# A Fourier-mixing and ELU kernel: batches 2 to 7 transformed from rows sorted by s mod 8, with the sums on VectorE

## The chip, the cores and the metric

One core of one Trainium2 chip. The metric is the device time of one execution in microseconds, lower is better. The engines are named as in the profile: PE is TensorE (matmul) and PEld its weight loads, DVE is VectorE, ACT is ScalarE, POOL is GpSimd, SP is SyncE, which here issues DMAs.

## What is computed

```python
batch, seq, dim = (8, 3008, 256)          # x, float32
X = np.fft.fft(np.fft.fft(x, axis=1), axis=2).real
h = X.reshape(8 * 3008, 256) @ w_in        # w_in  256 x 2048
g = np.where(h > 0, h, np.exp(np.minimum(h, 0)) - 1)
out = g @ w_out                            # w_out 2048 x 256
```

## The kernel before, in words

All products are float32, and each is two passes on PE. The transform over the 256 channels is multiplied into `w_in` once, which gives `Wc` (cosine part) and `Ws` (sine part). What is left of the first stage is the transform over the sequence, real and imaginary, of the channel-folded rows. Its results are written column by column (a column is one wave number) into rings `Rr` and `Ir` in SBUF, with `Rb` for one odd channel out. Wave numbers k and 3008 - k share their products: one gives the sum, the other the difference.

**The main loop.** The 8 x 1504 columns come in 47 tiles of `TW` = 256, and each tile in 8 slots, each of 256 of the 2048 hidden features: 376 slots. A slot is a fixed schedule: every piece of work is put in a list with a time in units of `T` = `PERIOD`, and the list, sorted by time, gives the order of instructions on every engine (`pin` keeps it). Slot s has, by offset from s T:

- 0: `mm_P`, two products of `Rr` into a PSUM bank H (PE).
- 0.87: `mm_X1` of slot s - 2, three products of the output matmul (PE). 0.9: `even_part`, which makes E from H, `Rb` and `wex` (DVE, line 1130).
- 2.17: `mm_Q`, two products of `Ir` added into H (PE). They add to what `even_part` reads, so they wait for E.
- 2.2 and 2.9: `g_plus`, `g_minus` of slot s - 1 (DVE, line 1160). From then on `sum_1`, `sum_3`, `sum_2`, `sum_4` of that slot run on POOL (line 576, out<-in G<-G): they are the sums of a Winograd form of the output matmul, which needs 7 products in place of 8.
- 3.04: `mm_X2`, `mm_X3` (PE). 3.55: `h_minus` (DVE, line 1144). 4.2 and 4.8: `below_plus`, `below_minus`, and in the next slot the two exponentials (ACT).
- Once in 8 slots: `comb_1` and `comb_2` at 4.2 (s mod 8 = 1), `comb_22` and `comb_3` at 1.0 and 2.5 (s mod 8 = 2), `turn_u` and `turn_v` at 4.2 (3 and 4), all on DVE, and the stores on SP's queue.

**The transforms.** Batch b covers 47 slots (`steps_b`), and while batch b - 1 goes through the main loop, batch b is loaded, folded and transformed; s0 = 47 (b - 1). Four tiles `xl0` to `xl3` take the rows s, 3008 - s, 1504 - s and 1504 + s, 6 rows to a partition. The folds (`fold_x`, line 664, on POOL in two halves each) first fold the channels, c with 256 - c (`e0` to `e3` the sums, `o0` to `o3` the differences), and then the four tiles with each other (`E0`, `E2`, `EO0`, `EO1`, `O0`, `O2`, `EO2`, `EO3`). In batches 2 to 7, `Mirror` uses rows paired by the mirror symmetry of 752: S and D, two more sums and differences on POOL, serve the odd rows of the even wave numbers. A transform has an even and an odd part, each a DFT of its own of 3 products into one bank H, put in at offset 4.75 of a slot, that is, between the slots on PE. In the next slot ACT copies a piece of it (`copy`), and DVE unfolds it (`unfold`) or joins even and odd into the ring (`plus`, `minus`), at offset 1.0, which is between E and g. There are 8 such parts a batch (real or imaginary, even or odd wave numbers, even or odd part), at s0 + 28, 30, 34, 36, 38, 40, 42 and 44. Matrices `MM` replace the earlier `MC` in the same tiles.

The helpers `mm` (line 567), `vtt` (573, DVE), `gtt` (576, POOL) and `act` (579) issue most instructions, so these lines stand for many places, and the names of the tiles tell them apart.

Of the kernel before, what the change touches and what calls it, by code (L numbers as in the profile page):

```python
# [17 lines left out]
SEQ = 3008  # L18
# [13 lines left out]
NC = (189, 188)  # L32
MW = (1417, 1786)
MOFF = (0, 1417, 3203, 4620)
# [42 lines left out]
def _row_pairs():  # L77
    p = np.arange(128)
    first = np.where(p < 96, 8 * p, 500 + 8 * (p - 96))
    second = np.where(p < 96, 750 - 8 * p, 250 - 8 * (p - 96))  # L80
    third = np.where(p < 64, 4 + 8 * p, 258 + 8 * (p - 64))
    return first, np.maximum(second, 0), third


def _used():
    p = np.arange(128)
    used = np.ones((128, 6), bool)
    used[94, 1:4] = False
    used[95, 0:4] = False
    used[:, 4] = used[:, 5] = p % 64 < 62  # L90
    return used


def _mirror_consts():

    rows = np.stack([r + o for r in _row_pairs() for o in range(2)], axis=1)
    used = _used()
    out = []
    for ri in range(2):
        fn = np.cos if ri == 0 else np.sin  # L100
        for kodd in range(2):

            def block(m, k, keep=None):
                s = rows[:, m : m + 1]
                w = np.where(s == 0, 0.5, 1.0) * used[:, m : m + 1]
                w = np.where(s == RUN, 0.5 if ri == kodd else 0.0, w)
                if keep is not None:
                    w = w * keep(s)
                return w * fn(2.0 * np.pi * ((s * k[None, :]) % SEQ) / SEQ)

            ka = 2 * np.arange(NA[kodd]) + kodd
            kc = 2 * np.arange(NC[kodd]) + kodd
            a = lambda m: block(m, ka, lambda s: s % 8 == 0)
            b = lambda m: block(m, ka, lambda s: s % 8 == 4)
            c = lambda m: block(m, kc, lambda s: s % 4 == 2)
            parts = [a(0), b(0), c(2), b(4), c(4)]
            if kodd:
                k = 2 * np.arange(NO) + 1
                parts += [block(m, k) for m in (1, 3, 5)]
            else:  # L120
                ev, od = 4 * np.arange(189), 4 * np.arange(188) + 2
                parts += [block(1, od if ri else ev), block(1, ev if ri else od)]
                parts += [block(5, ev), block(5, od)]
            out += parts
    return np.concatenate(out, axis=1).astype(np.float32)

# [35 lines left out]
def kernel(  # L162
# [14 lines left out]
    MM_dr = nc.inline_tensor(_mirror_consts(), name="mirror_mats")  # L177
# [27 lines left out]
    ix = cpool.tile([128, 7], I32, tag="ix")  # L205
# [51 lines left out]
    def mirror_table(c):  # L257

        for first, n, base in (
            ((0, 128, HALF - 1), (96, 32, HALF - 501)),  # L260
            ((0, 128, 750), (96, 32, 250)),
            ((0, 128, HALF - 5), (64, 64, HALF - 259)),
            ((0, 128, HALF - 1), (96, 32, HALF - 501), (0, 1, HALF - 2)),
        )[c]:
            pin(
                nc.gpsimd.iota(
                    ix[first : first + n, c + 3 : c + 4],
                    pattern=[[0, 1]],
                    base=base,
                    channel_multiplier=-8,  # L270
                )
            )
        if c == 1:
            pin(
                nc.vector.tensor_scalar(
                    out=ix[:, 4:5], in0=ix[:, 4:5], scalar1=0x3FF, scalar2=None,
                    op0=ALU.bitwise_and,
                )
            )

    def load_mirror(b):

        L = [
            spool.tile([128, 6 * ND], FP, tag=f"xl{j}", bufs=1, name=f"xl{j}")
            for j in range(4)
        ]

        def gather(j, pair):
            back = j in (1, 2)
            c = 3 if b == NB - 1 and j == 1 and pair == 0 else pair  # L290
            block = 2 - pair if back else pair
            pin(
                nc.gpsimd.indirect_dma_start(
                    out=L[j][:, 2 * block * ND : (2 * block + 2) * ND],
# [3 lines left out]
                        ap=ix[:, c + 3 : c + 4].bitcast(U32), axis=0  # L298
# [4 lines left out]

        def ahead(j):
            pairs = L[j].rearrange("p (m c) -> p m c", c=2 * ND)[:, 0::2]
            for p, q, row, gap in ((0, 64, 0, 4), (64, 96, 512, -254), (96, 128, 500, 14)):
                nc.sync.dma_start(
                    out=pairs[p:q],
                    in_=bass.AP(
                        tensor=xt,  # L310
                        offset=x.offset + (b * SEQ + (HALF if j else 0) + row) * ND,
                        ap=[[8 * ND, q - p], [gap * ND, 2], [1, 2 * ND]],
                    ),
                )

        def back(j):
            last = (SEQ if j == 1 else HALF) - 1
            cuts = (0, 80, 94, 128) if j == 1 else (0, 96, 128)
            for p, q in zip(cuts, cuts[1:]):
                s = 750 - 8 * p if p < 94 else 1018 - 8 * p  # L320
                nc.sync.dma_start(
                    out=L[j][p:q, 2 * ND : 4 * ND], in_=xrows(b, last - s, 8, q - p, 2)
                )

        loads = [
            lambda j=j, pair=pair: gather(j, pair)
            for j, pair in ((3, 1), (2, 0), (2, 2), (0, 1), (1, 0), (1, 2))
        ]
        loads += [
            lambda: ahead(3), lambda: back(2), lambda: ahead(0), lambda: back(1)  # L330
        ]
        return L, loads

# [201 lines left out]
    MM = {}  # L535

    def load_mirror_mats(ri, kodd):
        t = cpool.tile([128, BW], FP, tag=f"MC{ri}{kodd}", name=f"MM{ri}{kodd}")
        MM[ri, kodd] = t
        n = MOFF[2 * ri + kodd]  # L540
        nc.sync.dma_start(out=t[:, 0 : MW[kodd]], in_=MM_dr.ap()[:, n : n + MW[kodd]])

# [115 lines left out]
    def fold_x(L, engine_of, cuts_of, mirror=False, last=False):  # L658
# [36 lines left out]

        def first_row():

            if last:
                act(L[1][0:1, 4 * ND : 5 * ND], L[1][0:1, 5 * ND :])
            act(L[1][0:1, 5 * ND :], L[0][0:1, 0:ND])  # L700

        ops["x1", 0] = first_row
# [8 lines left out]
        if not mirror:  # L711
            return [E[1], E[3], O[1], O[3]], ops

        sd = []
        for n, t in ((0, E[1]), (2, O[1])):
            d = spool.tile([128, 380], FP, tag="side", bufs=2, name=f"sd{n}")
            sd.append(d)
            for m, f in ((0, ALU.add), (1, ALU.subtract)):
                op(
                    f"{'SD'[m]}{n}",  # L720
                    d[:, 128 * m : 128 * m + 128],
                    t[:, 128:256],
                    t[:, 384:512],
                    f,
                )
        return [(E[1], sd[0]), (E[3],), (O[1], sd[1]), (O[3],)], ops
# [5 lines left out]
    MIRROR_FOLDS = (  # L732
        "e0 c0 e3 c3 e2 c2 x1 e1 c1 E0 E2 EO0 S0 D0 o0 o3 o2 o1 O0 O2 EO2 S2 D2 EO1 EO3".split()
    )
# [59 lines left out]
    class Dft:  # L794
# [23 lines left out]

        def plus(self):
# [24 lines left out]
    def mirror_parts(ri, kodd, par):  # L844


        na, nc_ = NA[kodd], NC[kodd]
        if not par:
            return [
                (0, 0, 2 * na, 0),  # L850
                (2, 2 * na, nc_, 2 * na),
                (4, 2 * na + nc_, na + nc_, na),
            ]
        z = 3 * na + 2 * nc_
        if kodd:
            return [(2 * t + 1, z + t * NO, NO, 0) for t in range(3)]
        n = (188, 189) if ri else (189, 188)
        return [
            (6, z, n[0], 189 if ri else 0),
            (7, z + n[0], n[1], 0 if ri else 189),  # L860
            (5, z + NE, NE, 0),
        ]

    def of_tiles(tiles_):

        def stat(m):
            t, c = (tiles_[1], m - 6) if m > 5 else (tiles_[0], m)
            return t[:, 128 * c : 128 * c + 128]

        return stat  # L870

# [13 lines left out]
    def unfold_near(even, near, ab, ri, kodd, M, tt):  # L885


        na, nc_ = NA[kodd], NC[kodd]
        a, b, ab = even[0:M, 0:na], near[0:M, 0:na], ab[0:M]
        tt(ab[:, 0:na], a, b, ALU.add)  # L890
        p, q = (b, a) if ri else (a, b)
        tt(ab[:, steps_of(nc_ - 1, 94, -1)], p[:, 0:94], q[:, 0:94], ALU.subtract)

    def unfold_far(es, even, ab, ri, kodd, M, tt):
        na, nc_ = NA[kodd], NC[kodd]
# [6 lines left out]
    def join(es, odd, kodd, to, tt, ri=0, part=None):  # L902
# [7 lines left out]
        def run(t, start, step):  # L910
            return lambda i, z: t[:, steps_of(start + i * step, z - i, step)]
# [920 lines left out]
```

## Time and profile before

| | |
|---|---|
| median of 3 runs | 1935.96 us (1935.94 to 1936.14) |
| profiled execution, its own time | 1937.37 us |
| span from first to last instruction | 1934.6 us |
| granted TensorE clock | 1.000 |
| busy PE / PEld / DVE / ACT / POOL | 1923.9 / 1651.4 / 1305.2 / 864.3 / 1398.6 us |
| chain that ended last | PE 94%, DVE 3%, POOL 2%, ACT 1% |
| HBM read and written | 46.94 and 24.80 MB |

The busy time of an engine is the union of its instructions' times. PE's products overlap, so the time that one takes from the stream is read from start to start and not from its duration. A line of the timeline has start, duration, engine, line, operation, out<-in, shapes and count; several instructions in a row can be merged into one. In brackets stands the idle time before it and what ended it. A line of the groups has, after the shapes and the count, the busy time in us, the mean of one in ns, and the idle time before them with what ended it.

### The profile page before, as it was taken

The page shows a single profiled execution, that of the slowest core. Times are in us where ns is not written, and L with a number is a line of the kernel's source. Part 1 is how long each engine was busy: PE and PEld are TensorE (multiplying, and loading weights), DVE is VectorE, ACT ScalarE, POOL GpSimd, SP SyncE. Part 2 cuts the span into 40 slices and gives each one's busy share as a digit, 9 for nine tenths or more (in the row PEclk, how much of TensorE's full clock was granted, in tenths as well). Part 3 has the DMA queues.
Part 4 walks back from the last instruction along what each step waited for, and adds up shares of the span by engine and source line. Part 5 has one row for each costly group of instructions (what it writes and reads, how often), then busy time and mean ns, then how long its engine had stood idle before and what let it go on. Part 6 is the DMA issues. An engine that isn't in the chain of part 4 may idle for free.

```text
span 1934.6 us, 27221 instructions
## 1 busy us (share of the span) xinstructions
PE 1923.9 (99%) x8912; PEld 1651.4 (85%) x8912; DVE 1305.2 (67%) x2475; ACT 864.3 (45%) x1672; POOL 1398.6 (72%) x1860
## 2 busy tenths in 40 slices
PE   9999999999999999999999999999999999999999
PEld 6788788888888888888888888888888888888887
DVE  8876666766666666666666666676666666667666
ACT  5644444444444444444444444444444444444443
POOL 4888767876778777787677876778767876556555
PEclk9999999999999999999999999999999999999999
DMA  8146221111111111010110202012020110100101
GB/s 335 44 34 47 55 81 35 37 26 30 38 20 34 27 38 34 19 43 17 43 35 13 46 15 54 17 20 59 7 53 12 20 23 15 17 12 13 22 11 24
DMA packets 266141, 73.55 MB, mean 38 GB/s; under 512 B 249406, under 2 KB 250322, under 8 KB 266000
## 3 DMA queue, kind: packets, MB, share of 16 engines
q1 hardware_dynamic: 260048, 58.97, 15.6%
q0 software_dynamic: 3776, 12.59, 2.0%
q8 instruction: 70, 1.15, 0.2%
q14 instruction: 71, 0.58, 0.1%
q10 hardware_dynamic: 2176, 0.26, 0.1%
HBM read 46.94 MB, written 24.80 MB: 37 GB/s over the span
## 4 chain that ended last, share of the span: by engine, by line
PE 94%; DVE 3%; POOL 2%; ACT 1%; issue 1%; DMA 0%; DVEq 0%; POOLq 0%
PE H L567 37%; PE pB L567 16%; PE pC L567 16%; PE pD L567 16%; PE pA L567 8%; POOL WT L576 1%; POOL G L576 1%; DVE G L1160 0%; DVE E L1130 0%; DMA xl<-in_x_dram,ix 0%; DVE v L573 0%; DVE u L573 0%; DVE e L664 0%; POOL w L576 0%; DVE G L1144 0%
## 5 line engine op out<-in xcount | busy, mean ns | idle before, releaser
L576 POOL TENSOR_TENSOR G<-G 128x256 f32<-128x256 f32 x1440 | 1036.5, 730 | 479.9 <-DVE G L1160 364.1
L1130 DVE SCALAR_TENSOR_TENSOR E<-Rb,wex,H 128x256 f32<-128x256 f32 x752 | 327.9, 477 | 524.0 <-PE H L567 521.0
L579 ACT ACTIVATE G<-H 128x512 f32<-128x512 f32 x376 | 224.7, 598 | 958.1 <-DVE G L1144 953.5
L567 PE MATMUL H<-Ir,Ws 128*128 128x256 f32 x1504 | 387.4, 380 | 2.0 <-DVE E L1130 1.9
L567 PE MATMUL H<-Rr,Wc 128*128 128x256 f32 x1504 | 387.0, 380 | 0.8 <-DVE Ir L573 0.8
L567 PE MATMUL pC<-G,WT 128*128 128x256 f32 x1440 | 369.5, 379 | 0.0
L567 PEld LDWEIGHTS H<-Rr,Wc 128*128 128x128 f32 x1504 | 284.7, 190 | 52.2 <-issue 2.2
L567 PEld LDWEIGHTS H<-Ir,Ws 128*128 128x128 f32 x1504 | 278.5, 189 | 50.8 <-DVE E L1130 5.8
L567 PEld LDWEIGHTS pC<-G,WT 128*128 128x128 f32 x1440 | 273.6, 190 | 37.2
L1144 DVE SCALAR_TENSOR_TENSOR G<-E,H 128x512 f32<-128x512 f32 x376 | 257.1, 684 | 42.8 <-POOL G L576 4.0
L1160 DVE SCALAR_TENSOR_TENSOR G<-G,H 128x512 f32<-128x512 f32 x376 | 256.3, 682 | 43.1 <-ACT G L579 43.1
L1160 DVE SCALAR_TENSOR_TENSOR G<-M,G 128x512 f32<-128x512 f32 x376 | 257.3, 684 | 0.4 <-ACT M L579 0.4
L579 ACT ACTIVATE G<-G 128x512 f32<-128x512 f32 x376 | 233.3, 620 | 0.0
L567 PE MATMUL pB<-G,w 128*128 128x256 f32 x784 | 229.3, 379 | 0.0
L567 PE MATMUL pA<-G,w 128*128 128x256 f32 x784 | 229.2, 379 | 0.0
L567 PE MATMUL pD<-G,w 128*128 128x256 f32 x784 | 229.2, 379 | 0.0
L579 ACT ACTIVATE M<-G 128x512 f32<-128x512 f32 x376 | 224.0, 596 | 3.1 <-DVE G L1144 3.1
L579 ACT ACTIVATE M<-M 128x512 f32<-128x512 f32 x376 | 221.0, 588 | 0.1
L567 PE MATMUL pB<-G,WT 128*128 128x256 f32 x720 | 215.2, 380 | 1.3 <-POOL G L576 0.9
L567 PE MATMUL pD<-G,WT 128*128 128x256 f32 x720 | 214.2, 379 | 0.0
L567 PEld LDWEIGHTS pA<-G,w 128*128 128x128 f32 x784 | 149.0, 190 | 20.5
L567 PEld LDWEIGHTS pB<-G,w 128*128 128x128 f32 x784 | 148.9, 190 | 20.3
(163 smaller groups left out, 1433.8 us busy)
## 6 DMA issues: line engine op xcount, KB each, us to landing
out_dram<-ot SPq DMA_DIRECT2D x496, 32.0 KB
xl<-in_x_dram SPq DMA_DIRECT2D x16, 256.0 KB
out_dram<-ot SPq DMA_DIRECT2D x256, 2.0 KB
Rb<-r SPq DMA_DIRECT2D x10, 376.0 KB
raw<-in_moe_w_in_dram SPq DMA_DIRECT2D x7, 512.0 KB
xl<-in_x_dram SPq DMA_DIRECT2D x24, 128.0 KB
MC<-dft_mats SPq DMA_DIRECT2D x3, 943.5 KB
xl<-in_x_dram SPq DMA_DIRECT2D x4, 512.0 KB
```

The lines of the kernel that those rows point to most:

```text
L567: nc.tensor.matmul(out_, lhsT=lhsT, rhs=rhs, start=start, stop=stop, skip_group_check=True)
L576: pin(nc.gpsimd.tensor_tensor(out=o, in0=a, in1=b, op=op))
L579: pin(nc.scalar.activation(out=o, in_=i, func=func, **kw))
L1130: nc.vector.scalar_tensor_tensor(out=S.E[:, c], in0=Rb[:, cols(i)], scalar=wex[:, f : f + 1], in1=S.H[:, c], op0=ALU.mult, op1=ALU.add,)
L1144: nc.vector.scalar_tensor_tensor(out=two(S.G[:, 0:512])[:, :, ::-1], in0=two(S.E), scalar=2.0, in1=two(S.H), op0=ALU.mult, op1=ALU.subtract,)
L1160: nc.vector.scalar_tensor_tensor(out=o, in0=e, scalar=-1.0, in1=h, op0=ALU.add, op1=ALU.max)
```

## The change

Batches 0 and 1 keep their transforms. For batches 2 to 7:

- Rows are loaded 8 to a group, sorted by s mod 8: m = 0 to 3 from the near half group (`far` = 0, 96 partitions) and m = 4 to 7 from the mirrored one (`far` = 1, 94 partitions), 4 rows of 1 KB to a partition. Each tile `xl` is filled twice a batch, near and then far. Two of the four loads of each round are gathers on POOL's queue, the other two go by SP (one or two issues).
- The folds of the channels stay on POOL, in 32 pieces of 256 elements, one in each slot from s0 - 4 to s0 + 27; ACT writes the edge channel of each e piece.
- The eight sums between the tiles go to DVE (`quarter_sum`): near pieces as one 96x512 instruction, far ones as two 94x256.
- On DVE too, `quarter_pairs` combines the row classes (1, 7), (3, 5) and (2, 6), each as 94x128: sum and difference for even wave numbers, and for odd ones a rotation by a per-row tangent (`twist_tab`), whose cosine is in the matrix. These take the place of S and D, which are left out.
- A transform's even and odd parts become 4 products each: even parts of 94 or 95 columns each, odd parts of 188 or 189, on 94 to 96 rows. The even part had 663 columns (even wave numbers) or 658 (odd), the odd part 754 or 1128.
- On the way back, the parts for odd wave numbers are spread by sums and differences of neighbours (`spread`); `unfold` has 6 instructions in place of 4, and for odd wave numbers the odd part gets an ACT copy and two DVE instructions before `plus` and `minus`, which then read it from SBUF and not from PSUM.
- Sums and pairs are jobs of one slot each, at offset 4.25, behind `h_minus`. The slots with s mod 8 of 1, 3 or 4 are passed over. The transforms go to s0 + 30, 32, 34, 36, 37, 39, 42 and 44.

```diff
-    MIRROR_FOLDS = (
-        "e0 c0 e3 c3 e2 c2 x1 e1 c1 E0 E2 EO0 S0 D0 o0 o3 o2 o1 O0 O2 EO2 S2 D2 EO1 EO3".split()
-    )
+    UNITS = ((0, 96), (0, 96), (1, 94), (1, 94))
...
+    def quarter_fold(k, j, u):
+        far, n = UNITS[u]
+        src = state["L", j, far][0:n].rearrange("p (m d) -> p m d", d=ND)
...
+        o = unit(k, j, u)[0:n].rearrange("p (m o d) -> p m o d", o=2, d=64)
+        if k == "e":
+            gtt(o, lo[:, :, ::-1], hi[:, :, ::-1], ALU.add)
+        else:
+            gtt(o, lo, hi, ALU.subtract)
...
+    def quarter_sum(key, far):
+        ko, jo, ka, ja, kb, jb, f = SUMS[key]
+        if not far:
+            vtt(state[ko, jo, 0][0:96], state[ka, ja, 0][0:96], state[kb, jb, 0][0:96], f)
+            return
+        for u in (2, 3):
+            vtt(unit(ko, jo, u)[0:94], unit(ka, ja, u)[0:94], unit(kb, jb, u)[0:94], f)
+
+    def quarter_pairs(ri, kodd):
...
+        for n, (m, far) in enumerate(((1, 7), (3, 5), (2, 6))):
+            a, b = slot(m), slot(far)
+            u = new[0:94, 128 * n : 128 * n + 128]
+            if kodd:
+                for i, o in ((0, u), (1, b)):
+                    c = 4 * n + 2 * ri + i
+                    pin(nc.vector.scalar_tensor_tensor(
+                        out=o, in0=b, scalar=twist_tab[0:94, c : c + 1], in1=a,
+                        op0=ALU.mult, op1=ALU.add))
+            else:
+                vtt(u, a, b, ALU.add)
+                vtt(b, a, b, ALU.subtract)
...
-    class Mirror(Dft):
+    class Quarter(Dft):
+        def parts(self, par):
...
+                order = (
+                    ((0, 94), (("u", 2), 95), (4, 94), (("v", 2), 95))
+                    if self.kodd
+                    else ((0, 95), (4, 95), ((u, 2), 95), ((v, 2), 94))
+                )
...
+        def spread(self, t, u, v, n):
+            M = self.M
+            vtt(t[0:M, 0 : 2 * n : 2], u[0:M, 0:n], v[0:M, 0:n], ALU.add)
+            p, q = (v, u) if self.ri else (u, v)
+            vtt(t[0:M, 1 : 2 * n : 2], p[0:M, 1 : n + 1], q[0:M, 1 : n + 1], ALU.subtract)
...
+        def copy_odd(self):
+            if self.kodd:
+                self.far = spool.tile([128, NH], FP, tag="anti", bufs=2, name="far")
+                act(self.far[0 : self.M, 0:189], self.odd[0 : self.M, 189:378])
+        def unfold_odd(self):
+            if self.kodd:
+                t = spool.tile([128, NE], FP, tag="bs", bufs=3, name="od")
+                self.spread(t, self.odd, self.far, 188)
+                self.odd = t
...
+        for n, j in enumerate((0, 3, 2, 1)):
+            at((s0 - 11 + n) * T + 0.2, lambda b=b, j=j: load_quarter(b, j, 0))
+            at((s0 + 6 + 2 * n) * T + 0.2, lambda b=b, j=j: load_quarter(b, j, 1))
...
+        jobs = [
+            (5, 0, ("E0", "E2")), (5, 0, ("EO0", "EO1")),
+            (13, 0, ("O0", "O2")), (13, 0, ("EO2", "EO3")),
+            (21, 1, ("E0",)), (21, 1, ("E2",)), (21, 1, ("EO0",)), (21, 0, 0),
+            (21, 1, ("EO1",)), (21, 0, 1),
+            (29, 1, ("O0",)), (29, 1, ("O2",)), (29, 1, ("EO2",)), (29, 1, 0),
+            (29, 1, ("EO3",)), (37, 1, 1),
+        ]
+        step = 0
+        for least, n, keys in jobs:
+            step = max(step + 1, s0 + least)
+            while step % 8 in (1, 3, 4):
+                step += 1
+            if isinstance(keys, tuple):
+                for k in keys:
+                    at(step * T + 4.25, lambda k=k, n=n: quarter_sum(k, n))
+            else:
+                at(step * T + 4.25, lambda n=n, keys=keys: quarter_pairs(n, keys))
+        for ri, kodd, step in ((0, 0, 30), (0, 1, 34), (1, 0, 37), (1, 1, 42)):
```

## The prediction

> **What bounds the kernel now.** I read the busy totals first, then the groups of costliest instructions, then one ordinary step in the timeline.
>
> ```profile
> PE 1923.9 (99%) x8912; PEld 1651.4 (85%) x8912; DVE 1305.2 (67%) x2475; ACT 864.3 (45%) x1672; POOL 1398.6 (72%) x1860
> L576 POOL TENSOR_TENSOR G<-G 128x256 f32<-128x256 f32 x1440 | 1036.5, 730 | 479.9 <-DVE G L1160 364.1
> L1130 DVE SCALAR_TENSOR_TENSOR E<-Rb,wex,H 128x256 f32<-128x256 f32 x752 | 327.9, 477 | 524.0 <-PE H L567 521.0
> ```
>
> TensorE (PE) has work in 99% of the span and VectorE (DVE) waits for it 521 us before E. So TensorE's own stream sets the end, and each microsecond taken from it counts, if nobody makes it wait. The same step on each engine (start, duration, engine, work):
>
> ```profile
> 527.53 1.03 PE L567 MATMUL H<-Rr,Wc 128*128 128x256 f32 x4
> 528.59 0.87 DVE L1130 SCALAR_TENSOR_TENSOR E<-Rb,wex,H 128x256 f32<-128x256 f32 x2 [1.85 <-PE H L567]
> 529.52 0.79 PEld L567 LDWEIGHTS H<-Ir,Ws 128*128 128x128 f32 x4
> 529.68 1.03 PE L567 MATMUL H<-Ir,Ws 128*128 128x256 f32 x4
> 530.21 3.03 POOL L576 TENSOR_TENSOR G<-G 128x256 f32<-128x256 f32 x4 [0.44 <-DVE G L1160]
> 530.80 0.69 DVE L1144 SCALAR_TENSOR_TENSOR G<-E,H 128x512 f32<-128x512 f32 x1
> 532.27 1.03 PE L567 MATMUL H<-Rr,Wc 128*128 128x256 f32 x4
> ```
>
> A step lasts 4.74 us (527.53 to 532.27): 22 passes of 256 columns, 215 ns each, 0.842 ns a column; a float32 product is two passes. The loop is tight at E: it ends at 529.46, the weight load that waits for it starts at 529.52, and the product at 529.68, just on time. E may be 0.05 us late; beyond that TensorE stops. VectorE's free window goes from the end of h (531.49) to the next E (533.34): 1.85 us. And GpSimd (POOL) adds the sums of G from 530.21 to 533.24, over nearly all of that window.
>
> [...] Today's recurring VectorE work has one of its two tensors in PSUM (H, M, pB, pC, pD); the change adds work with both in SBUF. [...] The pow instruction (two SBUF inputs) next to GpSimd, once second and once first, and rx beside a shape as wide with one PSUM input:
>
> ```profile
> 97.19 1.30 POOL L576 TENSOR_TENSOR w<-raw,w 128x512 f32<-128x512 f32 x1 [0.88 <-ACT w L579]
> 97.22 1.81 DVE L439 SCALAR_TENSOR_TENSOR pow<-raw,pow 128x512 int32<-128x512 int32 x1
> ...
> 114.75 0.68 DVE L439 SCALAR_TENSOR_TENSOR pow<-raw,pow 128x512 int32<-128x512 int32 x1
> 114.82 1.76 POOL L576 TENSOR_TENSOR w<-raw,w 128x512 f32<-128x512 f32 x1 [3.15 <-ACT w L579]
> ...
> L573 DVE TENSOR_TENSOR rx<-bs,side 8x375 f32<-8x375 f32 x1 | 1.3, 1336 | 0.0
> L573 DVE TENSOR_TENSOR Ir<-M,bs 127x375 f32<-127x375 f32 x1 | 0.5, 544 | 0.0
> ```
>
> Second, pow ends at 99.03, 0.54 us after GpSimd's end (98.49); first, it takes 0.68 and GpSimd's w takes 1.76 instead of 1.30. Who takes the next turn matters too:
>
> ```profile
> 220.06 1.54 POOL L576 TENSOR_TENSOR G<-G 128x256 f32<-128x256 f32 x2
> 220.89 2.45 DVE L573 TENSOR_TENSOR rx<-bs,side 8x377 f32<-8x377 f32 x3
> 221.56 1.31 POOL L664 TENSOR_TENSOR e<-e,e 128x384 f32<-128x384 f32 x1
> ```
>
> The first rx (1114 ns in its group) ends 0.40 us after the sum that ends at 221.60, then GpSimd's e goes, then the second rx (1336 ns) ends 0.40 us after e (222.87). They take turns, so each further piece of VectorE's lets one waiting instruction of GpSimd in between. [...]
>
> **TensorE's part, batches 2 to 7.** Per real or imaginary half, today: even part 663 columns (wave numbers even) or 658 (odd), odd part 754 or 1128. Measured from first product to what follows: 1.12, 1.11, 1.27 (436.44 to 437.71) and 1.90 us. The last:
>
> ```profile
> 489.04 2.06 PE L567 MATMUL H<-MM,e 128*128 128x376 f32 x6
> 490.94 1.02 PE L567 MATMUL H<-Rr,Wc 128*128 128x256 f32 x4
> ...
> 34.51 0.52 PEld L567 LDWEIGHTS H<-pick,Ws 128*128 128x128 f32 x4 [0.36 <-ACT Ws L579]
> 34.95 0.52 PEld L567 LDWEIGHTS H<-Rr,Wc 128*128 128x128 f32 x3
> ```
>
> After: even parts are 4 products of 94 or 95 columns, 8 passes. 95 columns would be 0.08 us, but the loads of one-column products come 0.11 us apart (34.51 to 34.95, four), and that is the floor: 8 x 0.112 = 0.90. Odd parts are 4 products of 188 or 189 columns: 756 x 2 x 0.842 = 1.27. So even -0.22 and -0.21, odd 0 and -0.63: -1.06 a half, x 2 halves x 6 batches = **-12.7 us**. It comes in full, since it is TensorE's own time.
>
> **VectorE's part.** Added per batch: 16 jobs put behind h (4 of two 96x512 sums, 8 of two 94x256, 4 of six 94x128 pieces). Behind another, an instruction takes 0.085 us + 1.04 ns an element (four of 189: 1.12). That is 4 x 1.24 + 8 x 0.70 + 4 x 1.31 = 15.8 us[...]. Spreads and smaller unfolds add about 2.5 us. VectorE's share goes from 67% to about 74%, so in total it has room. By step it has not. With turns, in the step above:
> - two of 512: running sum ends 531.72, +0.54, GpSimd's next +0.62 (0.74 less the overlap seen above), +0.54 = 533.42. Late by 0.08: about nothing. Without GpSimd it would end at 532.7.
> - two of 256: 531.72 + 0.27 + 0.62 + 0.27 = 532.88. In time by 0.46.
> - six of 128: 531.72 + 0.14 + 0.62 + 0.14 + 0.62 + 0.14, then three free at 0.22 = 534.04. Late by 0.70, TensorE stops about 0.6.
>
> A job may lie in a step with comb_22 and comb_3 (step mod 8 = 2), where 0.97 us of the window is gone, or with an unfold ahead of h (0.9 to 1.7 us gone). Where a transform follows in the same step, its 0.9 to 1.27 us of TensorE cover the delay. Placing the list over the steps of the six batches (s0 mod 8 = 7, 6, 5, 4, 3, 2):
> - 24 jobs of six pieces: 10 plain x 0.55, 4 with an unfold x 1.7, 5 with comb x 1.05, 5 covered: 17.8
> - 24 of two 512: 18 free, 6 with comb x 0.75: 4.5
> - 48 of two 256: 10 with an unfold x 0.5, 6 with comb x 0.2, 3 with both x 1.1, the rest free: 9.5
> - steps without a job: longer unfolds, two es of 188 and two ring sums of 376 that now read SBUF twice, GpSimd late for sum_2: 10 x 0.45: 4.5
>
> Sum 36.3; of TensorE's waits today on E, Ir and G (1.9, 0.8 and 0.9 us) about 3 lie in the same places and are replaced: **+33 us**.
>
> **What costs nothing.** GpSimd loses 16 halves of sums (1.0 us), 4 of S and D and 2 of 6 gathers, and gets 32 folds of 256 (estimate 0.85, from 1.19 at 384) for 16 of 384: about -12 us a batch, hidden in its 480 us of idle time. Its G sums slip by a turn (0.5), inside over 1 us before X1 reads blk 2. ScalarE gets 16 edge copies (0.2 by the nearest small row) and 2 copies of half a transform (0.35); it idles over 1.5 us where they stand. Transfers: SP's issues of x fall from 11 to 6 a batch, near rows are asked for 7 steps (33 us) and far rows 6 steps (28 us) ahead of their folds, and the DMA engines are 14% busy. If loads were late, GpSimd and then the sums would slip: 0 to 5 us, taken as 0.
>
> **Sum.** -12.7 + 33 = +20 against the profiled execution's 1937.4 us: 1957.7, and as its own time stands 1.4 above the median of 1936.0, **1956.5** for the runs.
>
> **Rivals.**
> - Faster: the read clash does not bite TensorE (VectorE keeps its turn over consecutive instructions, or GpSimd yields). Then only stalls from VectorE's own length remain, about 12 us by the same list (six pieces or 512 with comb, six pieces with an unfold): -12.7 + 12 - 3 = -4, 1932. It decides once all stalls together are under 15.7 us (12.7 and the 3 replaced), against 36.3 here. For it: 67% load. Against it: the turns seen at 220 to 223 us.
> - GpSimd keeps its chain of four, and VectorE gets in only at 533.24: the jobs end 0.5 (256) to 1.1 (512, six pieces) late: 48 x 0.46 + 48 x 1.08, and 10 for comb and unfolds, 84 us of stalls: 2004. For it: one pow of 2302 ns, which sat through two GpSimd instructions. Against it: the rx rows.
> - The change doesn't shorten TensorE: short products paying their full load (8 x 0.19 = 1.52 instead of 0.90, x 24 = +15). Excluded by the 0.11 spacing.
>
> **Numbers.** Main case 0.75, with 1942 to 1975 for its own range (a stall a third less or more, loads late); GpSimd keeping its chain 0.11; faster 0.12; about even 0.02. 80%: 1938 to 1992, which leaves out the faster case and the upper part of the second. A difference under 0.2% can't be told from none here.
>
> **What would show it.** Right: DFT even parts near 0.90 us and odd parts 1.27; VectorE's sums well over 0.70 and six-piece jobs ending with GpSimd's sums; PE idle at H<-Ir,Ws waiting for E, some 30 us in all; batches longer by 3 to 4 us. Wrong: these sums at bare length beside GpSimd, or E's waits below 10 us.

## The result and the profile after

The changed kernel takes 1962.4 us (median of 4, 1961.4 to 1963.1) against 1936.05: ratio 1.0133, 95% interval 1.0115 to 1.015. It is slower by 26 us; 1956.5 had been forecast, in a range of 1938 to 1992. The profiled execution has a span of 1960.0 us. The busy totals, two of the costliest groups and three groups of the new sums (the helpers' lines have moved: 576 is now 546, 573 is 543, 567 is 537; `even_part` went from 1130 to 1191):

```profile
PE 1924.9 (98%) x9008; PEld 1649.0 (84%) x9008; DVE 1492.1 (76%) x2834; ACT 880.1 (45%) x1782; POOL 1356.3 (69%) x1795
L546 POOL TENSOR_TENSOR G<-G 128x256 f32<-128x256 f32 x1440 | 1059.2, 745 | 550.3 <-DVE G L1221 438.7
L1191 DVE SCALAR_TENSOR_TENSOR E<-Rb,wex,H 128x256 f32<-128x256 f32 x752 | 327.1, 476 | 375.6 <-PE H L537 372.0
L543 DVE TENSOR_TENSOR QM<-QM,QM 94x256 f32<-94x256 f32 x48 | 45.3, 945 | 0.0
L543 DVE TENSOR_TENSOR e<-e,e 96x512 f32<-96x512 f32 x24 | 25.4, 1097 | 0.0
L543 DVE TENSOR_TENSOR o<-o,o 96x512 f32<-96x512 f32 x24 | 23.0, 994 | 0.0
```

VectorE is busy 187 us longer, and what it waited for TensorE before E has shrunk from 521 to 372 us. GpSimd's G sums got a little longer (730 to 745 ns). The waits of TensorE (waiter, releaser, total us, times, longest):

```profile
PE H L537 <- DVE E L1191: 25.3, 39, 1.8
PE pB L537 <- POOL G L546: 2.2, 9, 0.3
```

Before, the wait for E was 1.9 us in 3 places. The view starts a wait only once the last product's modelled end is past, so it shows less than the whole loss: the part before that end counts as busy. That is also why PE is busy for 1924.9 us, 1 us more than before although its work is shorter; without the new VectorE work the same 9008 products are busy for 1913.0 us (e2_no_jobs, below).

Starts show the loss better. In an ordinary slot the first product on `Ir` starts 2.16 us after the first one on `Rr`. Set slot by slot against the trace of e2_no_jobs, that distance grows in the changed kernel by 31.3 us in all, and the stretch from there to the next slot by another 4.4, mostly 0.1 us after a late start. Together that is 35.7 of the 35.8 us between the two profiled spans (1960.0 and 1924.2 us). It lies in 50 of the 96 slots that follow a job; all the other slots together differ by 0.1 us.

The transforms did become shorter. Timeline, PE, an even part and an odd part:

```profile
675.24 0.58 PE L537 MATMUL H<-QM,e 95*128 95x95 f32 x4
675.66 0.39 PE L537 MATMUL H<-QM,pairs 94*128 94x95 f32 x2
675.88 0.39 PE L537 MATMUL H<-QM,QM 94*128 94x94 f32 x2
676.10 0.63 PE L537 MATMUL H<-Rr,Wc 128*128 128x256 f32 x2
...
708.81 0.81 PE L537 MATMUL H<-QM,pairs 94*128 94x189 f32 x4
709.45 0.48 PE L537 MATMUL H<-QM,QM 94*128 94x189 f32 x2
709.77 0.48 PE L537 MATMUL H<-QM,e 94*128 94x189 f32 x2
710.10 0.38 PE L537 MATMUL H<-Rr,Wc 128*128 128x256 f32 x1
```

From first product to the next slot's: 0.86 us (0.90 forecast) and 1.29 (1.27). A weight load of 128 columns on 94 rows takes 191 ns, as long as one on 128 rows (190); loads of 64 columns on 128 rows take 136. And this is a six-piece job in a plain slot, with VectorE, GpSimd and TensorE together:

```profile
652.92 3.16 POOL L546 TENSOR_TENSOR G<-G 128x256 f32<-128x256 f32 x4 [0.80 <-DVE G L1221]
653.52 0.69 DVE L1205 SCALAR_TENSOR_TENSOR G<-E,H 128x512 f32<-128x512 f32 x1
654.12 0.36 DVE L543 TENSOR_TENSOR pairs<-e,QM 94x128 f32<-94x128 f32 x1
654.52 0.77 DVE L543 TENSOR_TENSOR QM<-e,QM 94x128 f32<-94x128 f32 x1
655.22 0.28 DVE L543 TENSOR_TENSOR pairs<-e 94x128 f32<-94x128 f32 x1
655.52 0.70 DVE L543 TENSOR_TENSOR e<-e 94x128 f32<-94x128 f32 x1
656.04 0.89 POOL L546 TENSOR_TENSOR QM<-xq 94x256 f32<-94x256 f32 x1
656.15 0.93 DVE L543 TENSOR_TENSOR pairs<-e,QM 94x128 f32<-94x128 f32 x1
657.11 0.29 DVE L543 TENSOR_TENSOR QM<-e,QM 94x128 f32<-94x128 f32 x1
657.32 0.86 DVE L1191 SCALAR_TENSOR_TENSOR E<-Rb,wex,H 128x256 f32<-128x256 f32 x2
658.24 1.13 PE L537 MATMUL H<-Ir,Ws 128*128 128x256 f32 x4 [0.93 <-DVE E L1191]
```

Six equal pieces take 0.28 to 0.93 us each; one that is not held up takes 0.28 (the third and the sixth). The other four sat through an instruction of GpSimd: the first, second and fourth through G sums, the fifth through the fold (656.04 to 656.93) that followed the four sums. E started at 657.32, where 656.05 would have been in time (the slot's products on `Rr` start at 654.99), and TensorE stood still: its products on `Ir` came at 658.24, 3.25 us after those on `Rr`, which is 1.09 us late. So E could be 0.18 us late for nothing, not 0.05 as the prediction had it.

### The profile page after: what moved, and what is told of

It reads as the page before. It is cut to its first block, busy times and chain, and to the rows that moved or that the text cites. A ratio compares the mean times of both kernels' runs of the same rounds, so it can differ in the third digit from the quotient of the medians.

```text
span 1960.0 us, 27767 instructions
## 1 busy us (share of the span) xinstructions
PE 1924.9 (98%) x9008; PEld 1649.0 (84%) x9008; DVE 1492.1 (76%) x2834; ACT 880.1 (45%) x1782; POOL 1356.3 (69%) x1795
## 4 chain that ended last, share of the span: by engine, by line
PE 80%; DVE 15%; POOL 3%; issue 1%; ACT 1%; DMA 0%; DVEq 0%; POOLq 0%
PE H L537 33%; PE pC L537 14%; PE pD L537 14%; PE pB L537 13%; PE pA L537 7%; DVE E L1191 3%; DVE G L1221 2%; DVE G L1205 2%; POOL G L546 1%; DVE QM L543 1%; DVE pairs L764 1%; DVE o L543 1%; DVE v L543 1%; DVE QM L764 1%; POOL WT L546 1%
## 5 line engine op out<-in xcount | busy, mean ns | idle before, releaser
L546 POOL TENSOR_TENSOR G<-G 128x256 f32<-128x256 f32 x1440 | 1059.2, 745 | 550.3 <-DVE G L1221 438.7
L537 PE MATMUL H<-Ir,Ws 128*128 128x256 f32 x1504 | 391.5, 383 | 25.7 <-DVE E L1191 25.3
```

The costliest lines, as they stand in the source:

```text
L537: nc.tensor.matmul(out_, lhsT=lhsT, rhs=rhs, start=start, stop=stop, skip_group_check=True)
L546: pin(nc.gpsimd.tensor_tensor(out=o, in0=a, in1=b, op=op))
```

## The experiments

All are edits of the changed kernel; lines left out of the code are marked by three dots. A "job" is the added VectorE work of one slot. My theory: VectorE's jobs, with two SBUF inputs, take turns with GpSimd's sums, so E is late and TensorE waits. Rivals: VectorE simply has too much work in a slot; or the longer way back (spreads, unfolds, ring sums) makes the loss.

**e1_psum_input: the second input from PSUM.**

```diff
-            vtt(unit(ko, jo, u)[0:94], unit(ka, ja, u)[0:94], unit(kb, jb, u)[0:94], f)
+            vtt(unit(ko, jo, u)[0:94], unit(ka, ja, u)[0:94], H[0:94, 0:256], f)
```

(and the same in the near sums and the pairs, with H the bank of the slot)

> The changed kernel, but every VectorE job (the sums and the pairs) reads its second input from the PSUM bank H of its slot and not from SBUF: same instructions, lengths, slots and order, no new wait, other values (the sums between tiles are left out of the result). Read clash (my theory: an instruction of VectorE with two SBUF inputs takes turns with GpSimd's G sums, so E is late): the jobs fall to bare length (96x512 from about 1.05 us to 0.62 to 0.69, 94x256 from 0.54 to 0.95 to 0.35 to 0.42), TensorE's wait for E falls from 25 us to under 10, and the time to 1930 to 1938. Rival, VectorE simply has too much work behind h: nothing changes in length, 1958 to 1963.

Measured: 1948.0 us, between the two ranges. The group rows of VectorE say why:

```profile
L543 DVE TENSOR_TENSOR QM<-QM,H 94x256 f32<-94x256 f32 x48 | 19.6, 409 | 0.0
L543 DVE TENSOR_TENSOR o<-o,H 96x512 f32<-96x512 f32 x24 | 15.4, 680 | 8.0 <-ACT G L549 8.0
L543 DVE TENSOR_TENSOR e<-e,H 94x256 f32<-94x256 f32 x24 | 10.0, 418 | 15.9 <-ACT G L549 15.9
```

The instructions are at bare length, 409 and 680 ns (in the trace before, sums of 512 with one input in PSUM take 681 to 687), where the changed kernel has 945 (QM<-QM,QM) and about 1050 in the mean of the two 96x512 rows. So the long durations come with the second SBUF input, which the rival (no change in length) denies. But the first of each job now waits 0.67 us (8.0 us over 12 jobs) for ScalarE's reading of the same bank, which the expectation had ruled out. The experiment put a wait in place of the one it removed, so its time does not say what the lengths are worth. e5 was made for that.

**e2_no_jobs: without the sums and the pairs.**

```diff
+            if isinstance(keys, tuple):
+                continue
...
-            u = new[0:94, 128 * n : 128 * n + 128]
...
+            u = a
```

> The changed kernel without the VectorE jobs (the sums between tiles and the pairs are left out; the transforms read the folded pieces as they are). Products, loads, folds and the way back stay. Read clash and VectorE's length alike: the 12.7 us of TensorE come in nearly whole, 1924 to 1930. Rival, the way back (spreads, longer unfolds, ring sums that read SBUF twice) makes the loss: 1945 or more.

Measured: 1925.9 us, ratio 0.9944 (0.9928 to 0.9961) to the kernel before, which took 1936.6 in the same set of runs. The busy totals, and TensorE's wait for E:

```profile
PE 1913.0 (99%) x9008; PEld 1653.1 (86%) x9008; DVE 1318.7 (69%) x2546; ACT 879.9 (46%) x1782; POOL 1329.6 (69%) x1795
PE H L537 <- DVE E L1178: 2.7, 6, 1.2
```

The products' gain arrives nearly whole, and the way back costs little: it is not the cause. All of the 36.5 us from here to 1962.4 belong to the jobs.

**e3_behind_E: the jobs behind E.**

```diff
-                    at(step * T + 4.25, lambda k=k, n=n: quarter_sum(k, n))
+                    at(step * T + 1.03, lambda k=k, n=n: quarter_sum(k, n))
```

(and the same for the pairs)

> The changed kernel with each job at offset 1.03 of its slot (behind E, ahead of g_plus) in place of 4.25 (behind h). There GpSimd is idle, since its G sums wait for g. Nothing is left out. Read clash: the sums run at bare length (0.35 to 0.42 for 94x256, 0.62 to 0.69 for 96x512), TensorE's wait for E falls to a third, its wait for GpSimd's G sums grows (they start up to 1.3 us later, with about 1.5 us to spare), 1928 to 1945. Rival, VectorE's length: the work per slot is the same, E is as late as before, 1955 to 1965.

Measured: 1964.3 us. TensorE's waits:

```profile
PE pB L537 <- POOL G L546: 14.8, 41, 0.9
PE pD L537 <- DVE v L543: 5.1, 7, 1.5
PE H L537 <- DVE E L1191: 2.7, 6, 1.2
PE pA L537 <- DVE G L1221: 2.4, 6, 0.5
```

E is in time again (2.7 us, as in e2_no_jobs), as expected, but the time isn't better and the expected 1928 to 1945 are missed: what the jobs delay now is g, then GpSimd's G sums, and the X products wait for those. The 1.5 us that I had counted as spare were not enough. The jobs aren't at bare length either, since GpSimd's fold, and at times its last G sum, still met them: the two 96x512 rows have 1035 and 785 ns. The time lies in the rival's range (1955 to 1965), but the rival's reason, E as late as before, does not hold. Of the two places tried, each delays what comes next in the chain h, E, g.

**e4_sums_on_pool: the sums and plain pairs on GpSimd.**

```diff
-            vtt(unit(ko, jo, u)[0:94], unit(ka, ja, u)[0:94], unit(kb, jb, u)[0:94], f)
+            gtt(unit(ko, jo, u)[0:94], unit(ka, ja, u)[0:94], unit(kb, jb, u)[0:94], f)
```

(and the same for the near sums and the plain pairs)

> The changed kernel with the eight sums and the plain pairs on GpSimd in place of VectorE, at the same offsets; the rotations stay on VectorE. Nothing is left out. GpSimd gets some 28 us a batch more (8 x 1.3, 16 x 0.73, 12 x 0.46), about 83% of a batch. Read clash: E's waits fall to those of the rotations (12 jobs, under 10 us); in the near slots GpSimd has 6.5 us of work in a step of 4.74, so X1 waits for its G sums: 1930 to 1950. Rival, VectorE's length: also faster than 1962. The run tells what moving the sums back is worth; it does not tell the two apart by its time alone.

Measured: 2017.0 us, where 1930 to 1950 had been expected: a miss.

```profile
PE pB L537 <- POOL G L546: 57.4, 59, 2.9
PE H L537 <- DVE E L1191: 13.1, 15, 1.8
```

GpSimd has room in total (73% busy), but offset 4.25 lies between `sum_3` (3.6) and `sum_2` (4.4), and X1 waits for `sum_2`. Two sums of 96x512 take 2.5 us there (1267 ns each). Where they are put was wrong, so the run doesn't tell what GpSimd could bear.

**e5_one_input: one SBUF input and no other reader of H.**

```diff
-            vtt(unit(ko, jo, u)[0:94], unit(ka, ja, u)[0:94], unit(kb, jb, u)[0:94], f)
+            one(unit(ko, jo, u)[0:64], unit(ka, ja, u)[0:64])
```

(`one` issues `nc.vector.transpose`, which has a single input; the same for the near sums and the pairs. The widths are kept; the far pieces and the pairs take 64 partitions in place of 94.)

> The changed kernel, but each VectorE job instruction is a block transpose of one piece in SBUF (the sums and pairs are left out of the result): one SBUF input in place of two, same places, slots and widths, and, other than in e1_psum_input, no reader of bank H that has to wait for ScalarE. A transpose of 512 took 704 ns against 684 for a sum. Read clash: jobs at bare length (512: 0.70, 256: 0.45, 128: 0.3, less when one follows another), TensorE's stalls fall from about 40 us above those without jobs to about 10: 1932 to 1940. Rival, VectorE's length (e1_psum_input's 1948 taken at its word): 1945 to 1962.

Measured: 1929.5 us, faster than the 1932 to 1940 expected. The same count of VectorE instructions, of the same widths in the same slots, costs 3.5 us on top of e2_no_jobs, not 36.5. The busy totals, two of VectorE's groups, and TensorE's wait for E:

```profile
PE 1914.3 (99%) x9008; PEld 1651.8 (86%) x9008; DVE 1413.2 (73%) x2834; ACT 880.2 (46%) x1782; POOL 1329.6 (69%) x1795
L739 DVE STREAM_TRANSPOSE QM<-QM 64x256 f32<-64x256 f32 x48 | 18.9, 394 | 0.0
L739 DVE STREAM_TRANSPOSE e<-e 96x512 f32<-96x512 f32 x24 | 15.5, 683 | 0.0
PE H L537 <- DVE E L1179: 4.2, 11, 1.2
```

So **some 33 of the 36.5 us are the clash over SBUF reads**, and VectorE's length by itself is worth about 3.5. The stand-ins are as long as the bare sums of e1_psum_input (683 and 680 ns for 512; 394 to 430 and 409 to 418 for 256), but a piece in place of a rotation takes 260 to 304 ns, where a bare rotation takes some 340, so the length is worth a little more than 3.5, by an amount that no run shows. VectorE was busy 1413 us here and 1492 in the changed kernel: nearly all of these 79 us it spent sitting through GpSimd's instructions. The rival of too much work in a slot falls as the main cause.

**e7_sums_only and e8_pairs_only: which jobs.** e7 leaves the pairs out (`u = a`), e8 the sums (`pass` in place of `quarter_sum`), each with the others in their slots.

> The changed kernel with the pairs left out (the four six-piece jobs a batch; the result lacks them), the twelve jobs of two sums in their slots. By the prediction's list the sums cost 4.5 (512) and 9.5 (256) us on top of e2_no_jobs' 1925.9: 1938 to 1942. If the sums cost more than half of the 36 us: 1945 or more.

> The changed kernel with the sums left out and the six-piece jobs in their slots. By the prediction's list the six-piece jobs cost 17.8 us on top of 1925.9: 1942 to 1946. In the changed kernel's trace a plain six-piece job (slot at 650) made TensorE wait 0.93 us where the list has 0.55, because a fold of GpSimd took one more turn: so the upper end, or up to 1949.

Measured: 1938.8 us, as expected, and 1949.7, just above the 1949 given as the most. Over e2_no_jobs the sums cost 12.9 us and the pairs 23.7, together 36.6, which is the whole: the parts add up. (The four runs of e8 spread from 1949.0 to 1950.7; by the changed kernel's own trace, read from start to start as above, its six-piece jobs cost 22.8 us and its sums 12.9.) TensorE's wait for E, first without the pairs and then without the sums:

```profile
PE H L537 <- DVE E L1178: 7.5, 20, 1.2
```

```profile
PE H L537 <- DVE E L1191: 20.3, 24, 1.8
```

**e6_replaced: the same work in other slots.** The slots come from the prediction's arithmetic of one step, applied to each batch's own place in the 8-slot cycle.

```diff
-            while step % 8 in (1, 3, 4):
-                step += 1
...
+        for piece, step in zip(PIECES, PLACES[b]):
+            if piece[0] == "p":
+                at(
+                    (s0 + step) * T + 4.25,
+                    lambda p=piece: quarter_pairs(p[1], p[2], p[3]),
+                )
             else:
-                at(step * T + 4.25, lambda n=n, keys=keys: quarter_pairs(n, keys))
+                at((s0 + step) * T + 4.25, lambda p=piece: quarter_sum(*p))
```

(`PIECES` are 8 near sums, 8 far sums and 12 twos of pairs; `PLACES[4]`, for one, starts 8, 9, 11, 23 for the near E0, E2, EO0 and EO1)

> The changed kernel with the same VectorE instructions on two SBUF inputs at the same offset 4.25, but in other slots: one sum of 512 or one pair of 256 to a slot, six-piece jobs cut into twos, none of 512 in a slot with comb_22 or with an unfold, several together only where a transform follows in the slot and covers them. Nothing is left out. My theory (a job costs TensorE only what it makes E late, and each instruction waits at most one turn): stalls near those of e2_no_jobs, 1925 to 1932, faster than the kernel before. Rival, the clash itself costs time wherever it falls (GpSimd's sums late, X1 waits): 1940 to 1960.

Measured: 1931.25 us (median of 10), ratio 0.9975 (0.9966 to 0.9984) to the kernel before: **faster than both**, by 0.25% over the kernel before. TensorE waits 1.2 us for GpSimd's G sums (2.2 in the changed kernel), and for E:

```profile
PE H L537 <- DVE E L1195: 4.5, 11, 1.2
```

The busy totals and two of VectorE's groups:

```profile
PE 1915.8 (99%) x9008; PEld 1651.5 (86%) x9008; DVE 1482.5 (77%) x2834; ACT 880.0 (46%) x1782; POOL 1352.9 (70%) x1795
L543 DVE TENSOR_TENSOR e<-e,e 96x512 f32<-96x512 f32 x24 | 20.4, 848 | 0.0
L543 DVE TENSOR_TENSOR QM<-QM,QM 94x256 f32<-94x256 f32 x48 | 38.9, 811 | 0.0
```

VectorE is busy nearly as long as in the changed kernel (1482.5 us, for 1492.1 there and 1413.2 with one SBUF input), and the sums are still far above bare length: 848 and 811 ns, for 1097 and 945 in the changed kernel and 680 and 409 bare. So most of the clash is still there; what is nearly gone is its effect on E. That fits the account of one small job fitting into the window behind h, or being covered by a transform in the slot. Most of the 5 us left over e2_no_jobs is E again: in seven slots the products on `Ir` start 0.25 to 0.69 us later than there, 3.3 us in all.

## Why the prediction was right

The mechanism, its place and roughly the size held. The total came out closer than its parts: the jobs cost more than forecast, the rest less. Each term against its run:

- **TensorE, -12.7 us, in full.** Even parts 0.86 us for 0.90, odd 1.29 for 1.27; over all 48 parts, from first product to what follows, 64.9 us before and 51.6 after, so -13.3. With the 4.5 us listed for slots without a job, -8.2 us were forecast for all but the jobs; e2_no_jobs is 10.7 us below the kernel before (1936.6). So of the 4.5 some 2.6 came. The 3 us of today's waits that the prediction took as replaced did not go: the changed kernel still waits 0.8 us for `Ir` and 2.2 for GpSimd's G sums, and even e2_no_jobs waits 2.7 for E.
- **Turns.** The timeline above shows them, though not as strictly as forecast: four of the six pieces sat through one instruction of GpSimd each, and the third went right after the second. e5 shows that this clash, and not VectorE's length, is the main cost. The list for the rival without a clash had about 12 us of stalls from length, which was too much by a factor of three: e5 has 3.5 over e2_no_jobs. That it is the second SBUF input which counts had one contrast behind it in the trace before (rx 1336 ns beside Ir 544); e1 (945 to 409 ns) and e5 (1097 to 683) show it. Of the lengths in the list, 0.085 us + 1.04 ns an element, the trace before shows the second figure (346 ns at 188 elements, 540 at 376: 1.03 each); the 0.085 was my estimate from four of 189 in 1.12 us.
- **Sums: 4.5 + 9.5 = 14.0 us forecast, 12.9 measured** (e7).
- **Six-piece jobs: 17.8 us forecast, 23.7 measured** (e8). (The list itself adds up to 17.6.) This is the term that was mis-sized, and its excess is as large as the whole miss of 6 us. The step that failed is the price of such a job: the list counts the last three pieces as free at 0.22 us each, and has one price, 0.55 us, for every job in a plain slot. The changed kernel has nine of these. Three, with sums and differences and no fold behind them, make the products on `Ir` 0.44 us late. Three, with a fold of GpSimd in the next slot as in the timeline above, take one more turn: 1.09. Three, with rotations, take 0.81; a rotation's piece takes 0.34 to 0.35 us bare and not 0.28 (the timeline below this list). In all the plain jobs are late by 7.0 us, where the list has 5.5. Behind an unfold there are five jobs with 9.3 us in all, where the list has four with 6.8. The jobs with comb have 4.5 for 5.2, and those under a transform nothing, as forecast. The 0.1 us that follows each late start, 2.0 us here, is not in the list.
- **Costs set to nothing.** In e2_no_jobs, where loads, folds, edge copies and the way back all remain, the 2.6 us above are all that shows. There GpSimd's busy time fell by 69 us, close to the 72 that 12 us a batch would give. In the changed kernel it fell by 42: the G sums are 17 ns longer than in e2_no_jobs (745 for 728, 1440 of them), and that is 24 of the 27 us between.
- Of the rivals, "GpSimd keeps its chain of four" would have given 2004 and is excluded by the timeline above, where VectorE gets in among the four sums; "the read clash does not bite" by e5.
- Two small slips had little effect: the running G sum ends at 531.62 and not 531.72, and the sum gives 1956.3 and not 1956.5.

The end of a plain six-piece job of rotations in the changed kernel, with the products before and after it (2.98 us apart, 0.82 late):

```profile
1219.25 1.03 PE L537 MATMUL H<-Rr,Wc 128*128 128x256 f32 x4
1220.39 0.35 DVE L764 SCALAR_TENSOR_TENSOR o<-o,twist_tab 94x128 f32<-94x128 f32 x1
1220.66 0.34 DVE L764 SCALAR_TENSOR_TENSOR pairs<-QM,twist_tab,o 94x128 f32<-94x128 f32 x1
1221.04 0.35 DVE L764 SCALAR_TENSOR_TENSOR QM<-QM,twist_tab,o 94x128 f32<-94x128 f32 x1
1221.31 0.86 DVE L1191 SCALAR_TENSOR_TENSOR E<-Rb,wex,H 128x256 f32<-128x256 f32 x2
1222.23 1.13 PE L537 MATMUL H<-Ir,Ws 128*128 128x256 f32 x4 [0.66 <-DVE E L1191]
```

Left open: what GpSimd could bear if the sums were placed well in its own queue (e4 put them in the wrong place).

## What to carry to other kernels

An engine's busy share says whether work fits, not whether it fits there: ask which instruction is queued behind the added one, when that is due, and what the shared resource's other user does in that very window. Before moving work to VectorE, look at where its inputs lie; this kernel's recurring VectorE work had kept one tensor in PSUM, and the new work's second input in SBUF cost some 33 us here. A cost that can't be removed can be placed: the same instructions in other slots, mostly one to a slot or under a transform, turned 26 us of loss into 5 us of gain.

## What the runs showed that I had not expected

- A VectorE instruction that reads a PSUM bank right behind another waited 0.67 us for ScalarE's reading of the same bank, although both only read (e1_psum_input). The trace shows a wait on a semaphore of the program; what would happen without it no run shows.
- In the contest, VectorE pays more: its busy time grew by 79 us over e5_one_input, while GpSimd's 1440 sums grew by 24 us in all (728 to 745 ns).
- The gathers of 4 KB rows come in two kinds: those of 96 rows held GpSimd for some 0.92 us and those of 94 rows for 1.49 (e2_no_jobs, with no job beside them), against 0.97 for 128 rows of 2 KB in the kernel before. They also differ in which rows they fetch; which of the two makes the difference no run shows.
